# Decode attention on one core: a third buffer of transposed keys, paid for by giving up the second buffer of spread probabilities

## The chip, the cores and the metric

The kernel runs on one NeuronCore of one Trainium2 chip. The metric is device time in microseconds (us) of a whole execution. The kernel before took a median of 1345.64 us in three runs (1345.57 to 1347.1). The text names engines as the profile does: PE (TensorE), DVE (VectorE), ACT (ScalarE), POOL (GpSimd) and SP (SyncE, which issues the loads). Hardware facts come from these traces, or from the notes called the Trainium skill, and are then cited.

## The reference, cut to what matters

One decode step of four sequences. `A` is attention of one query per head over a cache of 8192 keys; `B` is a small gated MLP; a sigmoid gate mixes them.

```python
B, Sq, D = 4, 1, 1024          # one token for each of 4 sequences
H, Sk, Dh = 32, 8192, 128      # 32 heads, 8192 cached keys, bf16
q = (x @ wq) ...                                        # (B, H, 1, Dh)
scores = einsum("bhqd,bhkd->bhqk", q, k_cache) * Dh**-0.5
p = softmax(scores, axis=-1)
o = einsum("bhqk,bhkd->bhqd", p, v_cache)
a = o... @ wo
b = x + sigmoid(x @ w_r) * ((silu(x @ w_gate) * (x @ w_up)) @ w_down)   # [cut: top-1 of one token is that token]
out = g * a + (1 - g) * b,   g = sigmoid((x * gate_w).sum(-1))
```

`k_cache` and `v_cache` are 268 MB each (4 x 32 x 8192 x 128 x 2 bytes). Each cached byte is used once, for one query. The rest of the weights add 39 MB.

## The kernel before

The caches are walked in 32 "pairs" of keys and 32 of values; a pair is four heads, 8.39 MB, loaded into two of the five slots of a ring in SBUF, the core's on-chip memory. Four pairs make a group, which has one softmax. The order is K0 K1 K2 K3 (softmax 0) K4 V0 K5 V1 K6 V2 K7 (softmax 1) V3 K8 V4 and so on: values run four pairs behind keys. At the end, K31 (softmax 7), V27, V28, V29, V30, V31.

For keys, DVE transposes pieces of 32 keys in each partition into a tile `T`, eight per pair, and PE multiplies each `T` with the queries into `S_ps`. `T` comes from a pool of two buffers:

```python
ttp = ctx.enter_context(tc.tile_pool(name="ttp", bufs=2))
...                                                       # [cut]
for n in range(RD):                                       # RD = 8 pieces of a key pair
    T = ttp.tile([P, CJ, 2, 32, 2], BF, name="T", tag="T")      # 8 KB in each partition
    nc.vector.transpose(out=T..., in_=kn[:, c * CJ * Dh:(c + 1) * CJ * Dh]...)
    ...                                                   # 8 matmuls S_ps <- T, Z
    if n == JT:     flush()                               # finish an older group: PE
    if n == JT + 2: flush_late()                          # ... and its DVE steps
```

At the end of a group the softmax makes probabilities `PT`, which are spread with zeros between them into `PB`, so that one matmul serves four heads. `PB` is double: group g writes one while the last value pairs of group g-1 still read the other. The order on POOL: two copies into `PB`, and only then the all-reduce of the sums.

```python
PB = [const.tile([P, QP, 2, 2, 2, NQ, 4], BF, name=f"PB{i}") for i in range(2)]   # 8 KB each
...                                                       # [cut] inside softmax(g):
nc.scalar.activation(out=PTs[:], in_=sps[:]..., func=ACT.Exp, bias=negm[:, 0:1], ...)
nc.vector.transpose(out=PT[:]..., in_=PTs[:])
B_ = PB[g % 2]
for q in range(NQ):
    if q % 2 == 0: nc.scalar.copy(out=Bv[at, :, :, q, :], in_=Pv[at])          # ACT, 2 of them
    else:          nc.gpsimd.tensor_copy(out=Bv[at, :, :, q, :], in_=Pv[at])   # POOL, 2 of them
nc.vector.tensor_scalar(out=rex[:], ...)
nc.gpsimd.partition_all_reduce(tot[:], rex[:], ...)
def inverse(): nc.vector.reciprocal(out=rinv[:], in_=tot[:])    # DVE, a little later
late.append(inverse)
```

A value pair is 64 matmuls `o_ps <- ring, PB`, straight from the ring. After the fourth pair of a group, ACT and DVE copy `o_ps` out into `OS`:

```python
for c in range(RD):
    ...  nc.tensor.matmul(o_ps[row:row + NM, e, :], lhsT=B_[:, RD * t + c, z, w]..., rhs=vn[...], ...)
if t < GD - 1: return
nc.scalar.activation(out=o_sb[:], in_=o_ps[:, 0, :], ...)           # OS
nc.vector.scalar_tensor_tensor(out=o_sb[:], in0=o_ps[:, 1, :], ...)
```

Of the kernel before, what the change touches and what calls it, by code (L numbers as in the profile page):

```python
# [9 lines left out]
BF = mybir.dt.bfloat16  # L10
# [46 lines left out]
def kernel(  # L57
# [15 lines left out]
    nc = tc.nc  # L73
    P = 128
# [4 lines left out]
    NQ = 4  # L79
    QP = P // NQ  # L80
# [3 lines left out]
    RD = 2 * JT  # L84
# [14 lines left out]
    out2 = out.rearrange("b s d -> (b s) d")  # L99

    const = ctx.enter_context(tc.tile_pool(name="const", bufs=1))
    ttp = ctx.enter_context(tc.tile_pool(name="ttp", bufs=2))
    ptp = ctx.enter_context(tc.tile_pool(name="ptp", bufs=1))
    stat = ctx.enter_context(tc.tile_pool(name="stat", bufs=2))
    accp = ctx.enter_context(tc.tile_pool(name="accp", bufs=1, space=PSUM))
# [9 lines left out]
    def slots(n):  # L115
        at = turn[0]
        turn[0] = (at + n) % NS
        return at
# [3 lines left out]
    def load_pair(src, n, apart=False):  # L122

        a = slots(2)
        if a + 1 < NS and not apart:
            lo = a * RING
            nc.sync.dma_start(out=flat[:, lo:lo + 2 * n], in_=src)
            return [flat[:, lo:lo + n], flat[:, lo + n:lo + 2 * n]]
        halves = [ring[:, a], ring[:, (a + 1) % NS]]
        for i, half in enumerate(halves):  # L130
            nc.sync.dma_start(out=half[:, 0:n], in_=src[:, i * n:(i + 1) * n])
        return halves

    def small(shape, dtype=F32):
        return mps.tile(shape, dtype, name="small", tag="small")
# [29 lines left out]
    for he in range(4):  # L165
        half, e = divmod(he, 2)
# [28 lines left out]
    band(mq, QP, [(0, 1), (QP, NQ)])  # L195
    ZW = QP - 1 + P + 1
    Zt = [const.tile([P, 4, ZW], BF, name=f"Z{i}") for i in range(2)]
    PB = [const.tile([P, QP, 2, 2, 2, NQ, 4], BF, name=f"PB{i}") for i in range(2)]
    for z in Zt + PB:
        nc.gpsimd.memset(z[:], 0.0)  # L200

    OS = const.tile([P, 4 * Dh], F32)
# [128 lines left out]
    pending = []  # L331

    late = []

    def flush():
        while pending:
            pending.pop(0)()

    def flush_late():
        while late:  # L340
            late.pop(0)()

    def heads(d):
        return divmod(d * NQ, H)

    def kv_view(cache, d):
        b, h0 = heads(d)
        return cache[b, h0:h0 + NQ].rearrange("h (r j) d -> (h r) (j d)", j=2 * JR)
# [37 lines left out]
    def softmax(g):  # L386
        sps = S_ps.pop(g)
        m1 = stat.tile([P, 1], F32, tag="m1")
        nc.vector.tensor_reduce(out=m1[:], in_=sps[:].rearrange("p z n -> p (z n)"), axis=AX.X, op=ALU.max)  # L389
        mex = stat.tile([P, GH], F32, tag="mex")  # L390
        nc.vector.scalar_tensor_tensor(out=mex[:], in0=mask, scalar=m1[:, 0:1], in1=pen[:],  # L391
                                       op0=ALU.mult, op1=ALU.add)
        gmx = stat.tile([P, GH], F32, tag="gmx")
        nc.gpsimd.partition_all_reduce(gmx[:], mex[:], channels=P, reduce_op=bass_isa.ReduceOp.max)  # L394
        gmm = stat.tile([P, GH], F32, tag="gmm")
        nc.vector.tensor_tensor(out=gmm[:], in0=gmx[:], in1=nmask[:], op=ALU.mult)
        negm = stat.tile([P, 1], F32, tag="negm")
        nc.vector.tensor_reduce(out=negm[:], in_=gmm[:], axis=AX.X, op=ALU.add)  # L398
        PTs = ptp.tile([P, 1024], BF, name="PTs", tag="PTs")
        rs = stat.tile([P, 1], F32, tag="rs")  # L400
        nc.scalar.activation(out=PTs[:], in_=sps[:].rearrange("p z n -> p (z n)"), func=ACT.Exp, bias=negm[:, 0:1], scale=scale, accum_out=rs[:, 0:1])  # L401
        PT = ptp.tile([P, 32, 32], BF, name="PT")
        nc.vector.transpose(out=PT[:].rearrange("p j i -> p (j i)"), in_=PTs[:])  # L403
        B_ = PB[g % 2]
        Pv = PT[:].rearrange("p (q j) i -> p i q j", j=4)
        Bv = B_[:].rearrange("p i z w e s j -> p i (z w e) s j")
        for q in range(NQ):
            at = slice(QP * q, QP * (q + 1))
            if q % 2 == 0:
                nc.scalar.copy(out=Bv[at, :, :, q, :], in_=Pv[at])  # L410
            else:
                nc.gpsimd.tensor_copy(out=Bv[at, :, :, q, :], in_=Pv[at])  # L412
        rex = stat.tile([P, GH], F32, tag="rex")
        nc.vector.tensor_scalar(out=rex[:], in0=mask, scalar1=rs[:, 0:1], scalar2=None, op0=ALU.mult)  # L414
        tot = stat.tile([P, GH], F32, tag="tot")
        nc.gpsimd.partition_all_reduce(tot[:], rex[:], channels=P, reduce_op=bass_isa.ReduceOp.add)  # L416

        def inverse():
            rinv = stat.tile([P, GH], F32, name="rinv", tag="rinv")
            nc.vector.reciprocal(out=rinv[:], in_=tot[:])  # L420
            rinv_t[g] = rinv
        late.append(inverse)

    NM = 8 * NQ

    def v_pair(d):
        b, h0 = heads(d)
        g, t = divmod(d, GD)
        row = NM * t
        B_ = PB[g % 2]  # L430
        vv = kv_view(A_v_cache, d)
        if d < ND - 1:
            vs = load_pair(vv, RING, apart=d >= ND - 3)
        else:
            vs = [ring[:, slots(1)] for _ in range(2)]
            for half, cuts in ((0, 2), (1, 4)):
                for c in range(cuts):
                    lo, hi = c * RING // cuts, (c + 1) * RING // cuts
                    nc.sync.dma_start(out=vs[half][:, lo:hi], in_=vv[:, half * RING + lo:half * RING + hi])
        n = 0  # L440
        for c in range(RD):
            vn = vs[c // JT]
            for z in range(2):
                for w in range(2):
                    for e in range(2):
                        j0 = CJ * (c % JT) + 16 * z + 8 * w + 4 * e
                        nc.tensor.matmul(o_ps[row:row + NM, e, :],  # L447
                                         lhsT=B_[:, RD * t + c, z, w].rearrange("p e s j -> p (e s j)"),
                                         rhs=vn[:, j0 * Dh:(j0 + 4) * Dh], start=(n == 0), stop=(n == 4 * RD - 1),
                                         skip_group_check=True)  # L450
                    n += 1
                    if n == 4:
                        flush()
                    if n == 16:
                        flush_late()
        if t < GD - 1:
            return
        o_sb = OS
        nc.scalar.activation(out=o_sb[:], in_=o_ps[:, 0, :], func=ACT.Copy, scale=mE[:, 0:1])  # L459
        nc.vector.scalar_tensor_tensor(out=o_sb[:], in0=o_ps[:, 1, :], scalar=mE[:, 1:2], in1=o_sb[:],  # L460
                                       op0=ALU.mult, op1=ALU.add)

        def finish():
            oT = small([P, GH])
            for q in range(4):
                nc.tensor.matmul(oT[:, :], lhsT=o_sb[:, q * Dh:(q + 1) * Dh],  # L466
                                 rhs=selg[:, q].rearrange("p t s -> p (t s)"), start=(q == 0), stop=(q == 3))

            def scaled():
                hg = h0 + NQ - GH  # L470
                nc.vector.scalar_tensor_tensor(out=OT[:, hg:hg + GH, b], in0=oT[:, :], scalar=sgb[:, 1, b:b + 1],
                                               in1=rinv_t[g][:], op0=ALU.mult, op1=ALU.mult)
            late.append(scaled)
        pending.append(finish)
# [12 lines left out]
    for kind, d in order:  # L487
        if kind == "k":
            k_pair(d)
            if d in side:  # L490
                side[d]()
        if (kind, d) == ("v", ND - 1):
            for g in range(2):
                wo_block(g)()
        if kind == "v":
            v_pair(d)
        if (kind, d) == ("k", ND // 2):
            add_x()
        if (kind, d) == ("v", ND - 2):
            o_rows(0, GE)  # L500
    last = [wo_block(g) for g in range(2, NWB - 2)]
    last += [wo_block(g, r, r + FR // 2) for g in (NWB - 2, NWB - 1) for r in (0, FR // 2)]
    last.pop(0)()
    flush()
    flush_late()
    last.pop(0)()
# [38 lines left out]
```

## Time and profile before

| | before |
|---|---|
| median time | 1345.64 us |
| span of the profiled run | 1344.3 us |
| read from HBM (the chip's main memory) | 575.68 MB, 428 GB/s over the span |
| PE, DVE, ACT, POOL busy | 77%, 46%, 4%, 4% |
| DVE waiting for keys | 432 us |

These are lines of the profile's page of the kernel before. The rows `DMA` and `GB/s` cut the span into 40 equal slices: a 9 is a DMA busy share of 90% or more.

```profile
span 1344.3 us, 7989 instructions
PE 1040.5 (77%) x4536; PEld 224.8 (17%) x2348; DVE 618.1 (46%) x358; ACT 51.4 (4%) x46; POOL 58.6 (4%) x91
...
DMA  9999999999999999999999999999999999999997
GB/s 414 439 427 429 439 430 428 442 435 421 442 434 423 431 437 431 437 433 426 433 435 437 433 433 426 428 435 432 430 426 436 433 427 445 432 421 442 422 426 317
...
HBM read 575.68 MB, written 0.01 MB: 428 GB/s over the span
...
DMA 64%; PE 18%; DVE 11%; issue 7%; DVEq 0%; ACT 0%; SPq 0%
```

The last line is the chain of work that ended last, as shares of the span. No engine is full, but the DMA is, in every slice except the last. The page of the Trainium skill "DMA: Bandwidth & Descriptors", section "Where 436 GB/s comes from", puts the ceiling of the 16 ports at 435.2 GB/s. The trace comes close: in the steady middle, new keys end the wait in the chain at 678.19, 716.90, 755.67 and 794.38 us, 38.73 us apart on average, and in that time one key pair and one value pair arrive, 16.78 MB. That is 433 GB/s.

The next lines are from the table of who waited for whom, DVE only: instruction, what it waited for, total us, times, longest us.

```profile
DVE T L370 <- DMA ring<-in_A_k_cache_dram: 432.4, 30, 27.5
DVE OS L460 <- ACT OS L459: 70.9, 8, 19.9
...
DVE T L370 <- PE S_ps L376: 53.1, 35, 3.8
...
DVE rinv L420 <- POOL tot L416: 31.0, 7, 4.4
```

The transposes wait 432.4 us for keys and only 53.1 us for a `T` buffer to come free (that is what "`T` <- PE S_ps" means: the matmuls that read the old `T` are not done). The last lines are of the timeline at the end of the kernel, start and length in us; in brackets, how long the engine had been idle and what ended it. The first PE line is V27; the second is the start of V28 (`o_ps`, the next group); the others are later value matmuls. The ACT line is the last group's copies into `PB`.

```profile
1242.59 16.50 PE L447 MATMUL o_ps<-ring,PB 128*32 128x512 bf16 x64 [6.14 <-DMA ring<-in_A_v_cache_dram]
1262.04 3.23 PE L447 MATMUL o_ps<-ring,PB 128*32 128x512 bf16 x8 [2.94 <-DMA ring<-in_A_v_cache_dram]
...
1300.83 6.20 PE L447 MATMUL o_ps<-ring,PB 128*32 128x512 bf16 x28 [2.69 <-DMA ring<-in_A_v_cache_dram]
```

```profile
1241.56 3.83 ACT L410 COPY PB<-PT 32x1024 bf16<-32x1024 bf16 x2 [1.31 <-DVE PT L403]
```

V28 starts when its data has landed (2.94 us after V27 ends). Its `PB` had been ready since about 1245.4 us.

### The profile page before, as it was taken

To read this page: it belongs to the slowest core of one execution; us is meant where nothing else is said; L and a number is where in the kernel's file an instruction comes from. 1 tells how busy PE (TensorE), PEld (TensorE's weight loads), DVE (VectorE), ACT (ScalarE), POOL (GpSimd) and SP (SyncE) were. 2 spreads that over 40 slices of the span, in tenths; PEclk is the share of its full clock that TensorE was granted. 3 is DMA by queue.
4 is the path that set the end of the run, shared out by engine and by line. 5 is a ranking of instruction groups with operands and counts; after the bars stand their busy time and mean duration, and the time that the engine had idled before them with its cause. 6 is when DMAs were issued, how large, how long until landed. Compare 5 with 4: busy or idle time off the path is not lost.

```text
span 1344.3 us, 7989 instructions
## 1 busy us (share of the span) xinstructions
PE 1040.5 (77%) x4536; PEld 224.8 (17%) x2348; DVE 618.1 (46%) x358; ACT 51.4 (4%) x46; POOL 58.6 (4%) x91
## 2 busy tenths in 40 slices
PE   2565877777797777778977779697779679877998
PEld 0111111111111111111211112111111112111221
DVE  2555655535445554345455456146555154556000
ACT  0000100001000100001000010001000010000000
POOL 3000100001000100001000010000000010000000
PEclk9777988988998889899989889898899799889899
DMA  9999999999999999999999999999999999999997
GB/s 414 439 427 429 439 430 428 442 435 421 442 434 423 431 437 431 437 433 426 433 435 437 433 433 426 428 435 432 430 426 436 433 427 445 432 421 442 422 426 317
DMA packets 14175, 576.20 MB, mean 429 GB/s; under 512 B 1582, under 2 KB 1590, under 8 KB 2108
## 3 DMA queue, kind: packets, MB, share of 16 engines
q1 hardware_dynamic: 14132, 575.69, 99.4%
q8 instruction: 27, 0.44, 0.1%
q14 instruction: 8, 0.07, 0.0%
q10 hardware_dynamic: 8, 0.00, 0.0%
HBM read 575.68 MB, written 0.01 MB: 428 GB/s over the span
## 4 chain that ended last, share of the span: by engine, by line
DMA 64%; PE 18%; DVE 11%; issue 7%; DVEq 0%; ACT 0%; SPq 0%
DMA ring<-in_A_k_cache_dram 53%; DVE T L370 11%; PE S_ps L376 9%; PE o_ps L447 8%; DMA ring<-in_A_v_cache_dram 7%; DMA ring<-in_B_w_gate_dram 3%; DMA ring<-in_A_wo_dram 1%; PE o_ps L246 0%; PE acc L246 0%; DVEq L370 0%; PE acc L212 0%; PE small L466 0%; ACT OS L459 0%; ACT res L513 0%; SPq L142 0%
## 5 line engine op out<-in xcount | busy, mean ns | idle before, releaser
L370 DVE STREAM_TRANSPOSE T<-ring 128x2048 uint32<-128x2048 uint32 x256 | 570.7, 2282 | 496.1 <-DMA ring<-in_A_k_cache_dram 432.4
L376 PE MATMUL S_ps<-T,Z 128*128 128x512 bf16 x2048 | 528.6, 406 | 228.7 <-DVE T L370 228.5
L447 PE MATMUL o_ps<-ring,PB 128*32 128x512 bf16 x2048 | 461.5, 388 | 37.7 <-DMA ring<-in_A_v_cache_dram 37.7
L376 PEld LDWEIGHTS <-Z 128*128 128x128 bf16 x1024 | 105.1, 103 | 647.7 <-issue 639.4
L447 PEld LDWEIGHTS <-PB 128*32 128x32 bf16 x1024 | 100.9, 99 | 395.1 <-issue 371.2
L401 ACT ACTIVATE PTs<-S_ps,negm 128x1024 bf16<-128x1024 f32 x8 | 8.9, 1113 | 992.8 <-DVE negm L398 992.8
L353 POOL TENSOR_TENSOR Z<-qa,mq 128x16 bf16<-128x16 bf16 x32 | 9.0, 285 | 805.7 <-PE S_ps L376 724.1
L460 DVE SCALAR_TENSOR_TENSOR OS<-o_ps,mE,OS 128x512 f32<-128x512 f32 x8 | 6.0, 751 | 70.9 <-ACT OS L459 70.9
L412 POOL COPY PB<-PT 32x1024 bf16<-32x1024 bf16 x16 | 30.3, 1894 | 26.8 <-DVE rex L414 26.5
L410 ACT COPY PB<-PT 32x1024 bf16<-32x1024 bf16 x16 | 30.6, 1912 | 10.7 <-DVE PT L403 10.6
L309 DVE CAST LT<-small 128x64 bf16<-128x64 f32 x2 | 0.5, 225 | 43.3 <-PE small L307 43.3
L159 PE MATMUL small<-identb,x 6*128 6x6 bf16 x8 | 0.7, 200 | 23.1 <-DMA x<-in_A_x_dram 23.1
L394 POOL PARTITION_ALL_REDUCE gmx<-mex x8 | 3.2, 394 | 340.9 <-DVE mex L391 340.9
L389 DVE TENSOR_REDUCE m<-S_ps 128x1 f32<-128x1024 f32 x8 | 9.8, 1225 | 15.9 <-PE S_ps L376 15.9
L212 PE MATMUL acc<-ring,LT 128*4 128x512 bf16 x64 | 14.9, 378 | 1.9 <-DMA ring<-in_A_wo_dram 1.2
L420 DVE RECIPROCAL rinv<-tot 128x16 f32<-128x16 f32 x8 | 2.0, 248 | 31.0 <-POOL tot L416 31.0
L403 DVE STREAM_TRANSPOSE PT<-PTs 128x1024 bf16<-128x1024 bf16 x8 | 10.0, 1245 | 12.1 <-ACT PTs L401 12.1
L212 PE MATMUL acc<-ring,hT 128*4 128x512 bf16 x56 | 12.2, 379 | 0.0
L459 ACT ACTIVATE OS<-o_ps,mE 128x512 f32<-128x512 f32 x8 | 5.5, 687 | 120.1 <-PE o_ps L447 120.1
L466 PEld LDWEIGHTS small<-selg,OS 128*128 128x128 f32 x64 | 8.2, 191 | 3.8 <-issue 3.6
L246 PE MATMUL o_ps<-ring,xw 128*4 128x512 bf16 x56 | 5.1, 490 | 4.2 <-DMA ring<-in_B_w_gate_dram 4.2
L466 PE MATMUL small<-selg,OS 128*128 128x16 f32 x64 | 7.9, 255 | 0.0
(71 smaller groups left out, 76.0 us busy)
## 6 DMA issues: line engine op xcount, KB each, us to landing
ring<-in_A_k_cache_dram SPq DMA_DIRECT2D x14, 4096.0 KB
ring<-in_A_v_cache_dram SPq DMA_DIRECT2D x14, 4096.0 KB, 29.5
ring<-in_B_w_gate_dram SPq DMA_DIRECT2D x1, 7168.0 KB, 38.1
ring<-in_B_w_up_dram SPq DMA_DIRECT2D x1, 7168.0 KB, 37.7
ring<-in_B_w_down_dram SPq DMA_DIRECT2D x2, 3584.0 KB, 26.3
ring<-in_A_wo_dram SPq DMA_DIRECT2D x6, 1024.0 KB, 21.0
ring<-in_A_v_cache_dram SPq DMA_DIRECT2D x2, 2048.0 KB, 30.5
ring<-in_A_v_cache_dram SPq DMA_DIRECT2D x4, 1024.0 KB, 24.6
```

The costliest lines, as they stand in the source:

```text
L212: nc.tensor.matmul(out_ap, lhsT=lhsT, rhs=rhs, start=start, stop=True, skip_group_check=True)
L353: nc.gpsimd.tensor_tensor(out=Z[:, :, QP - 1:QP - 1 + P].rearrange("p e (q c) -> p e q c", c=QP)[:, :, :, 0], in0=qa[:, :, h0:h0 + NQ, b], ...
L370: nc.vector.transpose(out=T[:].rearrange("p j h i e -> p (j h i e)").bitcast(U32), in_=kn[:, c * CJ * Dh:(c + 1) * CJ * Dh].bitcast(U32))
L376: nc.tensor.matmul(sps[:, z, :], lhsT=Z[:, he, s:s + P], rhs=T[:, 16 * z:16 * z + 16, half, :, e], start=(t == 0 and n == 0 and he == 0), ...
L389: nc.vector.tensor_reduce(out=m1[:], in_=sps[:].rearrange("p z n -> p (z n)"), axis=AX.X, op=ALU.max)
L401: nc.scalar.activation(out=PTs[:], in_=sps[:].rearrange("p z n -> p (z n)"), func=ACT.Exp, bias=negm[:, 0:1], scale=scale, accum_out=rs[:, ...
L403: nc.vector.transpose(out=PT[:].rearrange("p j i -> p (j i)"), in_=PTs[:])
L410: nc.scalar.copy(out=Bv[at, :, :, q, :], in_=Pv[at])
L412: nc.gpsimd.tensor_copy(out=Bv[at, :, :, q, :], in_=Pv[at])
L447: nc.tensor.matmul(o_ps[row:row + NM, e, :], lhsT=B_[:, RD * t + c, z, w].rearrange("p e s j -> p (e s j)"), rhs=vn[:, j0 * Dh:(j0 + 4) * ...
L460: nc.vector.scalar_tensor_tensor(out=o_sb[:], in0=o_ps[:, 1, :], scalar=mE[:, 1:2], in1=o_sb[:], op0=ALU.mult, op1=ALU.add)
L466: nc.tensor.matmul(oT[:, :], lhsT=o_sb[:, q * Dh:(q + 1) * Dh], rhs=selg[:, q].rearrange("p t s -> p (t s)"), start=(q == 0), stop=(q == 3))
```

## The change

The intent: let the transposes run further ahead of the matmuls. A third `T` costs 8 KB in each partition. A build of the kernel before with three `T` buffers fails: the pool needs 24 KB in each partition and 21.9 KB are left. So the second `PB`, also 8 KB, is given up, and the copies into the one `PB` are moved behind the last value pair that reads the old contents. With that the all-reduce of the sums moves ahead of the copies in POOL's order.

```diff
-    ttp = ctx.enter_context(tc.tile_pool(name="ttp", bufs=2))
+    ttp = ctx.enter_context(tc.tile_pool(name="ttp", bufs=3))
-    PB = [const.tile([P, QP, 2, 2, 2, NQ, 4], BF, name=f"PB{i}") for i in range(2)]
+    PB = const.tile([P, QP, 2, 2, 2, NQ, 4], BF, name="PB")
     # softmax(g)
-        B_ = PB[g % 2]
-        for q in range(NQ):            # the four copies, two on ACT and two on POOL
-            ...
         nc.vector.tensor_scalar(out=rex[:], ...)
         nc.gpsimd.partition_all_reduce(tot[:], rex[:], ...)
         late.append(inverse)
+        def spread_p():
+            for q in range(NQ):        # the same four copies
+                ...
+        behind.append(spread_p)
     # v_pair(d)
+        if d == 0:
+            flush_behind()
     ...                                # [cut] the matmuls, now with PB in place of B_
         nc.vector.scalar_tensor_tensor(out=o_sb[:], in0=o_ps[:, 1, :], ...)
+        flush_behind()                 # after the fourth pair of a group
```

More of the change, by code (lines that the diff above doesn't have):

```diff
@@ L197 @@
     Zt = [const.tile([P, 4, ZW], BF, name=f"Z{i}") for i in range(2)]
-    PB = [const.tile([P, QP, 2, 2, 2, NQ, 4], BF, name=f"PB{i}") for i in range(2)]
-    for z in Zt + PB:
+    PB = const.tile([P, QP, 2, 2, 2, NQ, 4], BF, name="PB")
+    for z in Zt + [PB]:
         nc.gpsimd.memset(z[:], 0.0)
@@ L333 @@
     late = []
+    behind = []
     def flush():
@@ L337, in flush, with flush_behind @@
             pending.pop(0)()
+    def flush_behind():
+        while behind:
+            behind.pop(0)()
     def flush_late():
@@ L403, in softmax @@
         nc.vector.transpose(out=PT[:].rearrange("p j i -> p (j i)"), in_=PTs[:])
-        B_ = PB[g % 2]
-        Pv = PT[:].rearrange("p (q j) i -> p i q j", j=4)
-        Bv = B_[:].rearrange("p i z w e s j -> p i (z w e) s j")
-        for q in range(NQ):
-            at = slice(QP * q, QP * (q + 1))
-            if q % 2 == 0:
-                nc.scalar.copy(out=Bv[at, :, :, q, :], in_=Pv[at])
-            else:
-                nc.gpsimd.tensor_copy(out=Bv[at, :, :, q, :], in_=Pv[at])
         rex = stat.tile([P, GH], F32, tag="rex")
@@ L422, in softmax @@
         late.append(inverse)
+        def spread_p():
+            Pv = PT[:].rearrange("p (q j) i -> p i q j", j=4)
+            Bv = PB[:].rearrange("p i z w e s j -> p i (z w e) s j")
+            for q in range(NQ):
+                at = slice(QP * q, QP * (q + 1))
+                if q % 2 == 0:
+                    nc.scalar.copy(out=Bv[at, :, :, q, :], in_=Pv[at])
+                else:
+                    nc.gpsimd.tensor_copy(out=Bv[at, :, :, q, :], in_=Pv[at])
+        behind.append(spread_p)
     NM = 8 * NQ
@@ L429, in v_pair @@
         row = NM * t
-        B_ = PB[g % 2]
+        if d == 0:
+            flush_behind()
         vv = kv_view(A_v_cache, d)
@@ L447, in v_pair @@
                         nc.tensor.matmul(o_ps[row:row + NM, e, :],
-                                         lhsT=B_[:, RD * t + c, z, w].rearrange("p e s j -> p (e s j)"),
+                                         lhsT=PB[:, RD * t + c, z, w].rearrange("p e s j -> p (e s j)"),
                                          rhs=vn[:, j0 * Dh:(j0 + 4) * Dh], start=(n == 0), stop=(n == 4 * RD - 1),
```

## The prediction

> **What bounds the kernel now.** The stream of weights, keys and values from HBM. The page's third part gives 575.7 MB read in 1344.3 us, 428 GB/s; the table by stretches gives a DMA share of 0.98 to 1.03 in every 34 us stretch except the last (0.78). "DMA: Bandwidth & Descriptors" of the Trainium skill, section "Where 436 GB/s comes from", puts the ports' ceiling at 435.2 GB/s; the trace's 428 is within 2% of it. Compute has slack: PE is busy 77%, DVE 46%, and in the table of waits DVE waits 432 us for keys. The chain of waits is 64% DMA; its PE and DVE pieces are times when a load waited for its ring slot, but median issue to landing is 29.5 us for a V pair whose 8 MB take about 19.5 us at 430 GB/s (estimate), so loads are issued some 10 us before the queue would run dry.
>
> **What the change does.**
> 1. Third buffer of transposed keys: removes waits of the DVE transposes (2.27 us each) for S_ps matmuls: 53.1 us in total, 35 waits, longest 3.8. A key slot may come free 1 to 3 us earlier; the next load is issued earlier and queues longer. No bytes move sooner, as the DMA is never idle.
> 2. One PB buffer. The copies, two on ACT (1.91 us each) beside two on POOL (1.89 us each), now wait for the last V matmul of the previous group. In six groups of eight a key pair (about 18 us) lies between that matmul and the first reader of the new PB: hidden. In group 0 nothing is waited for. In the last group V pair 28 follows V pair 27 directly: it starts at 1262.0 us, 2.9 us after V pair 27 ends at 1259.1, because its data lands then. With the change ACT must do OS (0.7) and two copies (3.8) in between, so PE starts about 2 us later. PE waits 2.7 us for V data again at 1300.8 us, which absorbs most; the final loads are queued about 20 us ahead. At most 1 us reaches the end.
> 3. The all-reduce of the sums on POOL no longer stands behind the copies, so DVE's wait before the reciprocal (4.4 us, 7 times) goes. DVE's next transposes stand behind OS, which waits for the last V matmul anyway: no gain.
> 4. One memset of PB (3.5 us on POOL) goes, hidden under the first load.
>
> **On the critical path:** practically nothing. Sum: 0 to -1 us from a deeper queue, 0 to +1 us at the tail. I predict **1345.4 us**, range 1342.5 to 1348.5. Chances: faster by over 2% 0.01, within 2% 0.98, slower by over 2% 0.01.
>
> **What the profile would show.** DMA share about 1.0 in every stretch, 428 to 430 GB/s. DVE's waits for S_ps matmuls before T fall from 53 to under 15 us, its wait for keys rises by about as much, issue to landing of keys grows by 1 to 3 us. The last copies of PB start near 1260 us instead of 1241.5, V pair 28 near 1264 us, and PE's wait at 1300 us shrinks by 1 to 2 us. The reciprocal's 4.4 us wait is gone. The last 20 us look the same.
>
> **What would make it wrong.** If the DMA's rate depends on the queue's depth or on how key and value streams interleave, the time may move by some us. If the copies delay V pair 28 by 5 us or more, the slots of the last values and wo come free too late and the tail grows by that. A loss over 2% needs 27 us of idle DMA, which nothing here makes.

## More of the kernel before

The granted clock is the share of full TensorE speed that the chip's throttle allowed, as the profile reports it.

The order of instructions on PE, DVE and POOL is the program's; that of ACT and SP is left to the build.

## The result, and the profile after

| | before | after |
|---|---|---|
| median time | 1345.61 us (4 runs, 1344.53 to 1347.1) | 1345.95 us (4 runs, 1345.89 to 1346.29) |
| ratio, 95% interval | | 1.0002 (0.9985 to 1.002) |
| DVE waits for a free `T` | 53.1 us | not in the table |
| DVE waits for keys | 432.4 us | 483.5 us |
| V28 starts | 1262.04 us | 1263.83 us |

A ratio here is the mean time of one kernel's fast runs over that of the other's of the same rounds, so it is not quite the ratio of the two medians.

The page of the changed kernel, the lines that answer to those shown before:

```profile
span 1344.2 us, 7958 instructions
PE 1034.7 (77%) x4536; PEld 226.7 (17%) x2348; DVE 611.8 (46%) x358; ACT 50.6 (4%) x46; POOL 55.4 (4%) x90
...
DMA  9999999999999999999999999999999999999997
GB/s 414 437 430 429 440 428 428 444 433 418 446 430 426 432 435 432 438 429 432 430 435 433 437 435 424 431 430 435 433 425 441 431 426 442 431 424 427 434 424 313
...
HBM read 575.68 MB, written 0.01 MB: 428 GB/s over the span
...
DMA 66%; PE 13%; DVE 11%; issue 9%; ACT 0%; another core or an unknown queue 0%; DVEq 0%; SPq 0%
```

Same span, same bytes, same rate; in the chain PE's share fell by 5 points and nothing came of it. The table of DVE's waits:

```profile
DVE T L375 <- DMA ring<-in_A_k_cache_dram: 483.5, 36, 29.9
DVE OS L468 <- ACT OS L467: 102.4, 8, 20.1
...
DVE rinv L416 <- POOL tot L412: 4.1, 7, 0.6
```

Two waits went, and both came back under another name. The 53.1 us for a free `T` are gone and the wait for keys rose by 51.1 us: the transposes finish sooner and then stand before an empty slot. The 31.0 us before the reciprocal fell to 4.1 us, 26.9 us less, and the wait before `OS` rose by 31.5 us: DVE gets to `OS` sooner and waits there for the same value matmuls.

The end of the kernel, the same places as before:

```profile
1242.33 16.94 PE L455 MATMUL o_ps<-ring,PB 128*32 128x512 bf16 x64 [8.43 <-DMA ring<-in_A_v_cache_dram]
1263.83 3.57 PE L455 MATMUL o_ps<-ring,PB 128*32 128x512 bf16 x8 [4.55 <-ACT PB L426]
...
1269.15 38.41 PE L455 MATMUL o_ps<-ring,PB 128*32 128x512 bf16 x180
```

```profile
1259.31 0.69 ACT L467 ACTIVATE OS<-o_ps,mE 128x512 f32<-128x512 f32 x1 [21.61 <-PE o_ps L455]
1259.90 3.83 ACT L426 COPY PB<-PT 32x1024 bf16<-32x1024 bf16 x2
```

ACT now does `OS` and then the two copies, and V28 waits for them (4.55 us, ended by `ACT PB`), 1.8 us longer than before. The 2.69 us wait at 1300.83 us is gone in exchange: PE had that much to spare. One more comparison, made from the times at which SP issued the loads in the two traces: in the changed kernel the 39 loads of keys are issued 1.9 us earlier on average (up to 4.0), and the loads of the last values, after 1270 us, up to 4.5 us later. Neither moved the end, because loads queue in front of a DMA that is always busy.

### The profile page after: what moved, and what is told of

Same layout as the page of the kernel before. It is cut to its first block, busy times and chain, and to the rows that moved or that the text cites. A ratio compares the mean times of both kernels' runs of the same rounds, so it can differ in the third digit from the quotient of the medians.

```text
span 1344.2 us, 7958 instructions
## 1 busy us (share of the span) xinstructions
PE 1034.7 (77%) x4536; PEld 226.7 (17%) x2348; DVE 611.8 (46%) x358; ACT 50.6 (4%) x46; POOL 55.4 (4%) x90
## 4 chain that ended last, share of the span: by engine, by line
DMA 66%; PE 13%; DVE 11%; issue 9%; ACT 0%; another core or an unknown queue 0%; DVEq 0%; SPq 0%
DMA ring<-in_A_k_cache_dram 53%; PE o_ps L455 11%; DVE T L375 11%; DMA ring<-in_A_v_cache_dram 9%; DMA ring<-in_B_w_gate_dram 3%; PE S_ps L381 2%; DMA ring<-in_A_wo_dram 1%; ACT PB L426 0%; PE small L475 0%; PE acc L246 0%; DVEq L375 0%; ACT OS L467 0%; PE acc L212 0%; ACT res L522 0%
## 5 line engine op out<-in xcount | busy, mean ns | idle before, releaser
L375 DVE STREAM_TRANSPOSE T<-ring 128x2048 uint32<-128x2048 uint32 x256 | 566.6, 2277 | 494.9 <-DMA ring<-in_A_k_cache_dram 483.5
L381 PE MATMUL S_ps<-T,Z 128*128 128x512 bf16 x2048 | 520.2, 409 | 220.8 <-DVE T L375 220.3
L408 DVE STREAM_TRANSPOSE PT<-PTs 128x1024 bf16<-128x1024 bf16 x8 | 10.0, 1246 | 12.1 <-ACT PTs L406 12.1
L246 PE MATMUL S_ps<-ring,xw 128*4 128x512 bf16 x64 | 6.4, 590 | 0.3 <-DVE xw L161 0.3
## 6 DMA issues: line engine op xcount, KB each, us to landing
ring<-in_A_v_cache_dram SPq DMA_DIRECT2D x14, 4096.0 KB, 31.3
ring<-in_B_w_down_dram SPq DMA_DIRECT2D x2, 3584.0 KB, 27.8
```

Source lines behind the costliest of these rows:

```text
L246: nc.tensor.matmul(ps[32 * k:32 * k + Bn, z, :], lhsT=xT[TW * half + t], rhs=cols(w, t, 4 * z + k), start=(half + t == 0), stop=(half == 1 ...
L375: nc.vector.transpose(out=T[:].rearrange("p j h i e -> p (j h i e)").bitcast(U32), in_=kn[:, c * CJ * Dh:(c + 1) * CJ * Dh].bitcast(U32))
L381: nc.tensor.matmul(sps[:, z, :], lhsT=Z[:, he, s:s + P], rhs=T[:, 16 * z:16 * z + 16, half, :, e], start=(t == 0 and n == 0 and he == 0), ...
L408: nc.vector.transpose(out=PT[:].rearrange("p j i -> p (j i)"), in_=PTs[:])
```

## The experiments

Theory A: the stream from HBM sets the time, and everything in the change is hidden under it. Rival B: the third buffer gains some us and the late copies lose as many, and the two cancel. They need different tests: the parts alone, and the same change where the stream does not limit.

Three `T` beside two `PB` could not be built, for lack of space. With one `PB` the third buffer was tested by itself: the changed kernel and "one PB alone" differ in it and in nothing else. "Quarters" has it with the copies early. The kernels that compute a wrong result still passed the comparison with the reference. The attention term is evidently too small beside the tolerance to show missing values, so that pass says nothing about the attention of any kernel here.

### The changed kernel again, five rounds

> The changed kernel again, five rounds. Theory A (the DMA stream sets the time, both parts of the change are hidden under it): ratio to before 0.9985 to 1.0015, 1345 to 1347 us. Rival B (the third buffer of transposed keys gains some us and the late copies lose as many, and the two cancel): the same here; the next two runs tell them apart.

Measured: 1345.82 us (1345.68 to 1346.04), ratio 1.0002 (0.9989 to 1.0015). The next three ran on the same chip, against 1345.65 us of the kernel before (9 runs, 1344.87 to 1347.09).

### One PB alone

```diff
 # the changed kernel
-    ttp = ctx.enter_context(tc.tile_pool(name="ttp", bufs=3))
+    ttp = ctx.enter_context(tc.tile_pool(name="ttp", bufs=2))
```

> One PB with late copies, but two buffers of transposed keys as before. A: 1345 to 1347 us, within 1 us of the changed kernel; DVE's waits for S_ps matmuls before T back near 53 us; V pair 28 starts near 1264 us. B: slower than the changed kernel by 2 us or more, as the loss is left without the gain.

Measured: 1345.78 us (1345.09 to 1346.56), ratio 1.0002 (0.9989 to 1.0014). V28 starts at 1263.45 us, and DVE again waits for a free `T`:

```profile
DVE T L375 <- PE S_ps L381: 58.5, 40, 4.0
```

Without the third buffer there is no loss that it could have made good. B fails here, A holds. One thing does differ with the buffer: every run of the kernels with three `T` and full loads had a mean granted clock of 0.889 to 0.898, every run of this kernel and of the kernel before 0.909 to 0.919. PE waits for a transpose half as often (101 times in place of 199 in the first two profiles) and longer each time (220.3 and 228.5 us in all), so its pauses are bunched; whether that lowers the clock was not tested. It costs nothing here.

### Quarters: the copies early, the third buffer kept

V27 reads only the last quarter of `PB`. The other three quarters can be written at the softmax, and one buffer still does.

```diff
 # the changed kernel
-        def spread_p():
+        def spread_p(i0, i1):
     ...
-                    nc.scalar.copy(out=Bv[at, :, :, q, :], in_=Pv[at])
+                    nc.scalar.copy(out=Bv[at, i0:i1, :, q, :], in_=Pv[at, i0:i1])      # POOL likewise
     ...
-        behind.append(spread_p)
+        spread_p(0, QP - RD)
+        behind.append(lambda: spread_p(QP - RD, QP))
```

> The changed kernel, but three quarters of PB (the parts that the running V pair of the old group no longer reads) are written at the softmax as before, and only the last quarter behind the last V pair. The start of V pair 28 waits for no copy: about 1262 us in place of 1263.8. A: 1345 to 1347 us, within 1 us of the changed kernel. B: faster than the changed kernel and than before by 2 us or more.

Measured: 1344.93 us (1344.85 to 1345.17), ratio to before 0.9996 (0.9983 to 1.0008). V28 again waits for data and not for copies:

```profile
1260.91 3.06 PE L456 MATMUL o_ps<-ring,PB 128*32 128x512 bf16 x8 [3.99 <-DMA ring<-in_A_v_cache_dram]
```

The time is 0.9 us below the changed kernel's, and the two sets of five runs do not overlap, but the copies made at most a part of this. In the chains of the two profiled runs (this and the changed kernel's) the second wait for keys ends at 134.47 us here and at 135.16 us there, so the first 0.7 us are there before the first softmax (the first copies into `PB` start at 161 us). What makes them is open. At a wait for keys near 1144 us the gap is 0.5 us, and at the last loads of `wo` (1334.27 and 1335.27 us) 1.0 us, so up to half a microsecond may come from the copies or from the tail; that is not settled. The expected 2 us of B are not there.

### The last copies four times

How much may V28 be late before the end moves? The copies of the last group are done four times, with the same data.

```diff
 # the changed kernel
-            for q in range(NQ):
+            for q in list(range(NQ)) * (4 if g == ND // GD - 1 else 1):
```

> The changed kernel with the copies of the last group's PB done four times (same data), which puts 11.5 us more between V pair 27 and V pair 28. Reading 1 (what is left of slack is PE's own: from V pair 28 on PE waits for DMA only 0.4+0.4+0.6+0.6+0.3+0.2 = 2.6 us in the changed kernel): the time grows by 11.5 - 2.6 = about 9 us, to 1355. Reading 2 (the prediction's: the last loads are queued some 20 us ahead, so a delay of this size stays hidden): it grows by under 2 us.

Measured: 1349.96 us (1349.03 to 1351.71), ratio to before 1.0033 (1.0019 to 1.0047), 4.1 us above the changed kernel.

```profile
1275.21 3.29 PE L455 MATMUL o_ps<-ring,PB 128*32 128x512 bf16 x8 [16.13 <-ACT PB L426]
...
1338.97 7.07 PE L212 MATMUL acc<-ring,LT 128*4 128x512 bf16 x32 [0.36 <-DVE LT L309]
```

V28 starts 11.4 us late, as made. Neither reading had the size. From the start of V28 to the first transposes of the attention output PE needs 40.7 us against 43.4 us in the changed kernel, without any wait for data in either: in the 17 us from the start of V28 the granted clock was 0.92, and 0.75 in the changed kernel (why it came back sooner was not tested). From there to the last matmul it needs 3.9 us less (30.1 against 34.0), mostly as its waits for data, 2.6 us in the changed kernel, are gone. 11.4 - 2.6 - 3.9 = 4.9 us are left, and the profiled spans differ by 4.7 us. So the tail is PE's, as reading 1 has it: the loads queued ahead do not protect it. Reading 1 put what the tail can take up at 2.6 us; it took up some 6.5 us (2.6 + 3.9).

### Halved loads: the change where the stream does not limit

From the fourth pair on, each load brings only the first half of the columns of every 4096-element piece (except the very last value pair; the two before it are no longer split into two loads); all compute stays.

```diff
 # both kernels
+    def load_half(src): ...            # as load_pair, on views "p (c m) -> p c m", m cut to its first half
-        ks = load_pair(kv_view(A_k_cache, d), RING)
+        ks = load_half(kv_view(A_k_cache, d)) if d >= 3 else load_pair(kv_view(A_k_cache, d), RING)
-            vs = load_pair(vv, RING, apart=d >= ND - 3)
+            vs = load_half(vv) if d >= 3 else load_pair(vv, RING)
```

> The kernel before, with each load of keys and values from the fourth pair on cut to half of the columns of every 4096-element piece (wrong result on purpose; all compute stays). Takes the DMA limit away. Expected: 1050 to 1150 us, DMA share well under 0.9 and PE busy over 90% in the middle. If the time stays near 1345 us, the bytes were not what set it and theory A falls.

> The changed kernel with the same halved loads. If the third buffer is worth something where compute sets the pace (theory A with hidden gain): 30 to 60 us less than the halved kernel before, about 1.5 us for each of 32 key pairs. Rival C (the third buffer removes waits of an engine that is not the limit in any case): within 0.5% of the halved kernel before.

> One PB with late copies, two buffers of transposed keys, halved loads. The late copies alone should cost 0 to 5 us against the halved kernel before (only the last group has no key pair between old and new PB); if they cost over 10 us, the other groups are not hidden either.

Measured, three rounds each:

| halved loads | median us | ratio to the full kernel before |
|---|---|---|
| kernel before | 1202.12 (1201.55 to 1202.63) | 0.8932 |
| one PB, two T | 1175.63 (1174.92 to 1176.2) | 0.8735 |
| changed kernel | 1122.88 (1121.57 to 1125.26) | 0.8344 |

Fewer bytes alone take 144 us off, with all compute in place: the stream did set the time, which A needs. Freed of it, the change is worth 79 us. The third buffer by itself, with one `PB` in both kernels and the same order on ACT, is worth 52.8 us of that (1175.63 less 1122.88), in the range expected for the whole change. Two things were not as expected. The halved kernel before is 52 us slower than the top of its range (PE was busy 85% from 400 to 1000 us, not over 90%, with a DMA share of 0.70), and the late copies alone, which should have cost up to 5 us, gain 26.5 us. DVE's waits in the halved kernel before show why:

```profile
DVE PT L418 <- ACT PTs L416: 95.7, 8, 13.3
DVE rinv L435 <- POOL tot L431: 30.8, 7, 4.4
DVE OS L475 <- ACT OS L474: 17.2, 1, 17.2
```

In the full kernel before, `PT` waits 12.1 us for the exponentials; here 95.7 us, 13.3 us in each of seven groups. The build orders ACT by itself, and in all halved kernels of this set it put `OS` ahead of the next exponentials, so these waited for value matmuls. DVE's order then has rex, reciprocal, `OS`, transposes: the 4.4 us for the all-reduce behind the copies come on top, seven times. So these three are not quite the full kernels with fewer bytes. The next runs repair that, and test the 26.5 us by themselves.

### Halved loads, ACT in the program's order

```diff
 # both halved kernels
-    ctx.enter_context(tc.manual_schedule(engines={EngineType.PE, EngineType.DVE, EngineType.Pool}))
+    ctx.enter_context(tc.manual_schedule(engines={EngineType.PE, EngineType.DVE, EngineType.Pool, EngineType.Activation}))
```

> The kernel before with halved loads, and with the order of ACT's instructions fixed to the program's. (In the first halved kernels the build had put OS ahead of the exponentials on ACT, so that DVE waited 13.3 us for PTs in each of seven groups; in the full kernels the exponentials come first.) If that order cost what the trace says, about 7 x 13 us go, and the 4.4 us waits before the reciprocal hide under the V matmuls: 1070 to 1115 us.

> The changed kernel with halved loads and the same fixed order on ACT. Against hm_before only the third buffer should be left as a gain (about 53 us, as between the two halved kernels with one PB), less up to 5 us for the late copies of the last group: 45 to 55 us faster than hm_before, 4 to 5%. Rival: the gain of the first halved pair came from the order on ACT and POOL, and the two are within 10 us here.

Measured: kernel before 1144.79 us (1143.92 to 1146.06), changed kernel 1101.87 us (1099.81 to 1103.12), three rounds each, ratios to the full kernel before 0.8506 and 0.8188. The change gains 42.9 us, 3.7%, a little under the range expected. PE's waits for `T` in the two, first before, then after:

```profile
PE S_ps L391 <- DVE T L385: 117.3, 190, 10.5
```

```profile
PE S_ps L396 <- DVE T L390: 77.7, 84, 12.8
...
PE o_ps L470 <- POOL PB L443: 4.6, 1, 4.6
```

39.6 us of PE's waits for transposes go, and their number falls from 190 to 84; the late copies cost 4.6 us, once. That is the intent of the change, seen working, where PE sets the pace. The all-reduce's new place, also part of the change, is no likely rival here: DVE's wait before the reciprocal falls by 26.9 us (31.0 to 4.1) and its wait at `OS` rises by 27.0 us (50.7 to 77.7). That is read from the traces; no run tests it alone in this order of ACT. The rival of this run (the gain came from ACT's order) fails. The absolute time of the kernel before was mis-sized again, by 30 us beyond the range: fixing the order took the wait of `PT` from 95.7 to 12.1 us, but the wait of `OS` rose from 17.2 to 50.7 us, since DVE then waits at `OS` for the same matmuls. 83.6 - 33.5 = 50 us, and 57 us were measured.

### The all-reduce ahead of the copies, nothing else

```diff
 # the first halved kernel before: two PB, two T
+        nc.vector.tensor_scalar(out=rex[:], ...)              # moved up
+        nc.gpsimd.partition_all_reduce(tot[:], rex[:], ...)   # moved up
         for q in range(NQ):
             ...                                               # the four copies into PB
-        nc.vector.tensor_scalar(out=rex[:], ...)
-        nc.gpsimd.partition_all_reduce(tot[:], rex[:], ...)
```

> The first halved kernel before with only one thing changed: the all-reduce of the sums is issued on POOL ahead of the PB copies; two PB, two T. The late copies alone had made that halved kernel 26.5 us faster, against expectation. If that came from the reciprocal on DVE no longer waiting 4.4 us behind the copies in seven groups (30.8 us became 4.1): 1173 to 1179 us here too. If it came from the copies being late themselves: 1202 us, no gain.

Measured: 1174.30 us (1173.19 to 1177.01), ratio 0.873. That is the whole 26.5 us and a little more, with both `PB` still there. What the "one PB" version had gained was the all-reduce's new place, not the lateness of the copies.

### One buffer of transposed keys

```diff
 # the kernel before
-    ttp = ctx.enter_context(tc.tile_pool(name="ttp", bufs=2))
+    ttp = ctx.enter_context(tc.tile_pool(name="ttp", bufs=1))
```

> The kernel before with one buffer of transposed keys and full loads. If hiding depends on the depth: transposes and matmuls of a key pair alternate, 8 x (2.27 + 1.9 + about 0.4) = 36.6 us, and with 14 us of V matmuls a pair needs about 50 us against 39 us of loads, so compute sets the time: 1600 to 1700 us. If the depth never matters: 1345 us.

Measured: 1916.69 us (1914.5 to 1917.82), ratio 1.424, and the DMA is busy only 71.6% of the span. The direction is as expected, the size is 217 us beyond the range. This is the line of the S_ps matmuls on its page (busy us, mean ns; idle before them and for what):

```profile
L376 PE MATMUL S_ps<-T,Z 128*128 128x512 bf16 x2048 | 754.8, 532 | 602.1 <-DVE T L370 602.1
```

And these are two of the pieces in its timeline, eight matmuls each:

```profile
813.34 1.90 PE L376 MATMUL S_ps<-T,Z 128*128 128x512 bf16 x8 [2.40 <-DVE T L370]
...
838.09 3.57 PE L376 MATMUL S_ps<-T,Z 128*128 128x512 bf16 x8 [2.40 <-DVE T L370]
```

The estimate took 8 matmuls as 1.90 us. With a pause before every 8 they took up to 3.6 us: the granted clock was 0.757 on average, 0.917 in the kernel before, and the mean matmul rose from 406 to 532 ns. "TensorE: Matmul & The Clock Gate" of the Trainium skill, section "HAM oscillation — how this bites in real kernels", describes such a loss: idle gaps drop PE to half rate. Every pause of the stretch quoted, 809 to 847 us, is 2.4 us, shorter than the some 3.4 us that the section names as the rule, and the granted clock there was 0.73 all the same. (The build also changed ACT's order in some groups of this kernel; the 74 us that `PT` waited are in the number.) The dose is clear in any case: one buffer makes compute the limit, two hide it, a third has nothing left to hide.

### Half of the value matmuls, all of the bytes

```diff
 # the kernel before; wrong result on purpose
-                for z in range(2):
+                for z in range(1):
     ...
-                ... stop=(n == 4 * RD - 1)
+                ... stop=(n == 2 * RD - 1)
```

> The kernel before with full loads but half of the V matmuls left out (wrong result on purpose; every second group of 16 keys is not added). PE loses about 220 us of 1040 us of work. Theory A (bytes alone set the time): ratio to before 0.998 to 1.0015, at most the last 3 us of the tail gained. If PE's work mattered anywhere but at the end: 5 us or more faster.

Measured: 1347.77 us (five runs, 1345.03 to 1348.58) against 1345.30 us of the kernel before, ratio 1.0012 (0.9999 to 1.0024). PE's busy time fell from 1040.5 to 844.6 us, and nothing was gained; three of the five runs lost 2.5 to 3.3 us.

```profile
PE 844.6 (63%) x3512; PEld 179.1 (13%) x1836; DVE 617.4 (46%) x358; ACT 51.3 (4%) x46; POOL 58.5 (4%) x91
...
HBM read 575.68 MB, written 0.01 MB: 427 GB/s over the span
```

The profiled run is one of the three; its span is 2.5 us longer. Some 1.6 us of that come with the loads: they are already 1.5 us behind at the wait for keys that ends at 873.40 us here and at 871.87 us in the kernel before, and the data of the output projection's first matmuls land at 1329.62 against 1328.02 us. What held the loads up is open. The other 0.9 us are PE's: it now waits more, and the first matmuls of the output projection after its waits run at half rate.

```profile
1329.62 3.57 PE L212 MATMUL acc<-ring,LT 128*4 128x512 bf16 x8 [0.63 <-DMA ring<-in_A_wo_dram]
```

Eight of them take 3.57 us here; in the kernel before, eight took 1.89 us. The granted clock from 1310 to 1344 us was 0.85, against 0.99. This rests on one profiled run, and two of the five runs did not lose; the 0.12% are not settled.

## Why the prediction was right

**The bound.** Right. The rate stayed at 428 GB/s over the span with the DMA full in every slice but the last. Halving the cache loads took 144 us off with the same compute; taking 196 us of PE's work away took nothing off. "SBUF — State Buffer", section "Who interferes with whom", states that DMA does not contend with compute engines; the traces agree in that the rate was the same with 1040.5 and with 844.6 us of PE work (428 and 427 GB/s).

**Step 1, the third buffer.** Right in its effect: the 53.1 us became 51.1 us of waiting for keys, and the loads of keys were issued 1.9 us earlier, with no gain in time. One sign was wrong. The prediction said that issue to landing of keys would grow by 1 to 3 us; in the profile's view of the DMA the median for the largest set of key loads went from 35.5 to 35.0 us, and for value loads from 30.1 to 31.3 us. The ring explains part of it, by the code alone: with five slots and pairs of two, a key pair waits for the first half of the key pair before and the second half of a value pair, while a value pair waits for the second half of the key pair before. Earlier transposes therefore help value loads too: the first 35 of the 44 were issued 1.7 us earlier on average. The times of issue were the better witness than that median.

**Step 2, one PB.** Right: 1.8 us late at V28 (predicted about 2, start near 1264 us; measured 1263.83), absorbed at 1300 us. The reason given was half right. It was PE's idle time that absorbed the delay, and the "20 us of queued loads" would not have: with 11.4 us of delay the end moved by 4.1 us.

**Step 3, the all-reduce.** Right for this kernel: the wait moved from the reciprocal (26.9 us less) to `OS` (31.5 us more). It is no empty edit, though. With `OS` ahead of the exponentials on ACT and fewer bytes, the same move is worth 27.8 us (1202.12 less 1174.30, medians of two calls).

**Step 4, one memset less.** POOL's busy time fell from 58.6 to 55.4 us, and nothing else moved.

**The number.** 1345.4 us predicted, 1345.95 us measured, inside the range of 1342.5 to 1348.5. A forecast of no change that comes true says little about its steps by itself, as several errors of this size could cancel in it; the traces and the experiments carry them. The kernel had no gain to give: what it gained in slack it could not spend. Where compute sets the pace, the same edit is worth 42.9 us of 1144.8.

## What to carry to other kernels

Before widening a buffer, ask which wait ends last: a wait that a deeper buffer removes can come back almost whole (51.1 of 53.1 us here) in front of the engine or queue that really limits. Give up a second buffer freely where other work lies between its last reader and the next; look at the end of the kernel, where that work runs out. To learn what an edit is worth once a limit is gone, cut the limit (here, half of the bytes) and run both kernels so, but compare the order of instructions first, since a build that orders an engine by itself may have changed it.

## What the Trainium skill lacked or had wrong

- "TensorE: Matmul & The Clock Gate", section "HAM oscillation — how this bites in real kernels": it gives gaps over about 3.4 us as what makes PE cold. With pauses of 2.4 us before every 8 matmuls the granted clock was 0.73 (809 to 847 us, one buffer of transposed keys); over that whole run it was 0.757, and the matmuls took 532 ns on average instead of 406. So as a threshold this rule is too narrow; the section after it does tell of short idles between groups of matmuls, without a length.
- The same page: it has no word on a kernel that is slower for doing less on PE. With half of the value matmuls gone, the stretch from 1310 to 1344 us ran at a granted clock of 0.85 instead of 0.99, and 8 matmuls of the tail took 3.57 us instead of 1.89, after a pause of 0.63 us. That accounts for at most some 0.9 us of the 2.5 us that the profiled run lost; it is one profiled run, so not settled.
- "HBM Reference", section "Specifications (TRN2)": it gives about 358 GB/s effective for a core and about 425 GB/s for a core that streams alone. These runs, on one core, held 433 GB/s in the steady middle and 428 over the span, nearer to the 435.2 GB/s of the DMA page.
- No page has it: ACT's order was left to the build, and a change of the loads alone put `OS` ahead of the exponentials, with 95.7 us of waits before `PT` in place of 12.1.
